# Keys and queries of the later sequence blocks made in seven products per pair of tiles, with the projections in front of the mixers

## The chip, the cores and the metric

One Trainium2 chip; the kernel runs on one of its cores. The metric is the device time of one execution in microseconds. Three runs of the kernel before gave 523.54, 523.78 and 524.24 us; their median, 523.78 us, is the time before.

## What is computed

A sequence `x` of S = 2048 rows and D = 512 columns is normalized row by row (`xn`). Two branches read `xn`.

The first is linear attention with 32 heads of 16 columns. `q`, `k`, `v` are `xn @ wqkv`; `phi(t)` is `t + 1` where `t > 0` and `exp(t)` elsewhere, plus 1e-6:

```python
kv  = einsum("bhsd,bhse->bhde", phi(k), v)
z   = phi(k).sum over s
o   = (phi(q) @ kv) / (phi(q) . z + 1e-6)
s   = o @ wo
```

The second is a token mixer followed by an MLP: `h = gelu(layernorm(xn) @ w1)`, the four quarters of `h`'s columns are shifted by +1, -1, +2 and -2 rows, `x1 = xn + shifted @ w2`, and `x1 + gelu(layernorm(x1) @ w3) @ w4`, with F = 1376 inner columns. The output is `x + s * silu(second branch)`.

## The kernel before

**Tiles and stages.** The rows are cut into 16 tiles of 128 (`NT`), four tiles to a block (`QT = 4`, `NQ = 4` blocks). Each operand of a matrix product is held as a high part rounded to fp32r and a low remainder (`rounds`, `rounded`, L443 and L478), and a product of two operands is three matmuls, high-high, high-low and low-high (`products`, L470). A full-width matmul streams 512 columns.

The stages are, by the names of the tiles in the trace:

- *Projections.* `key(i)` (L748) makes one tile of keys from the transposed block `u` and the split weights `wk`: 4 chunks of 128 rows x 3 = 12 matmuls of 512 columns into the bank `k`. `feature_k` (L735) subtracts the row mean times the column sums of the weights (`wneg`), forms `phi` on ScalarE and VectorE, splits it, and adds it to the running key sum `zacc` by a DMA from GpSimd's queue. `query(i)` (L761) does the same with `wq` into the bank `q`, where `wq` was centered beforehand (`center`, L565), stores `relu` to DRAM from SyncE's queue (SP) and adds `exp` to it by a DMA from GpSimd's queue. `gram(i)` (L771) multiplies the normalized tile `x` with the key features into four accumulators `g` (12 matmuls).
- *Mixers.* `mix1(b, gg)` (L815, bank `h`, 12 matmuls each) makes a quarter of `gelu(.. @ w1)` for a block; `forms` (L836) makes the operands of the next product; `mix2(i)` (L871) multiplies with `w2` a pair of tiles at a time, in seven half-size products in place of eight (`seven`, L778, banks `pa`, `pb`, `pe`). The seven products share three banks: four of them go into `pb`, with read-outs by ScalarE or VectorE between.
- *Attention matrix*: `kv`, `m`, from `g`, `wv`, `wo`.
- *MLP*: `up_pair` (seven products, L1039), `down` (bank `acc`), and for the attention output `attend` and `attend_pair` (banks `s` and `pas`, `pbs`, `pes`), then `gate` and the store of the output.

**The order of the work.** The main function calls these pieces in program order, but it only records operations (`Plan.add`, L96). `Plan.emit` (L267) then lists them by a planner with a cost for each operation, a due time counted back from the matmul that needs it, a fixed number of buffers per kind (89 pieces `p`, four banks `mm`, four accumulators `acc`) and a rule for how long ahead of its due time an operation may take a buffer (`lead`, `early`). Each engine runs its list in order; semaphores hold it where data is missing. `SOONER` (L1402) is a table of operation numbers with corrections to their due times.

**Around the change**, the recorded order is: the weights `wk`, block 0 transposed, tiles 0 to 3; keys 0 to 3; `wq` centered; queries 0 to 3 and gram 0 to 3; `w1` loaded, centered and split (L1228); key 4. Then for blocks b = 1, 2, 3 (L1238): rows loaded and normalized, key and query of the block's tiles, and between them `mix1`, `forms` and `mix2` of the block *before* it. The mixer of block 3, the attention matrix and the MLP follow. A normalized tile `X[i]` stays in its buffer until `mix2` adds it to the mixer's output from GpSimd's queue (L882).

Of the kernel before, what the change touches and what calls it, by code (L numbers as in the profile page):

```python
# [85 lines left out]
class Plan:  # L86
# [180 lines left out]
    def emit(self, first, lead, reserve, window, ahead, table=()):  # L267
# [20 lines left out]
        while left:  # L288
# [5 lines left out]
            for e, cands in avail.items():  # L294
                picks = []
                low = INF
                for op in cands:
# [11 lines left out]
                    for t in fresh:  # L309
# [84 lines left out]
def linear_attn_gated_by_mixer(  # L394
# [29 lines left out]
    EARLY = (), ()  # L424
    AHEAD = 30.0, 20.0, 10.0, 0.0, 0.0
# [67 lines left out]
    onesr, bmask, tiny, zmore = fixed("onesr", P, F32R), fixed("bmask", P), fixed("tiny", 1), fixed("zmore", 1)  # L493
    hal = fixed("hal", NQ * NC * W)
    mv1, mv2 = fixed("mv1", 2 * NT), fixed("mv2", 2 * NT)
    rs1, rs2, ns1, nm1, nm2, au = (fixed(n, NT) for n in ("rs1", "rs2", "ns1", "nm1", "nm2", "au"))
# [13 lines left out]
    pool(.2, [], tiny.all, lambda: g.memset(tiny.all.get(), TINY))  # L510
    pool(.2, [], zmore.all, lambda: g.memset(zmore.all.get(), S * TINY))
# [84 lines left out]
    def scale_x(lo, n):  # L596

        r = rs1[:, lo:lo + n]
        w = small(f"w{lo}", n).all
        pl.ts(w, var(mv1, lo, lo + n), EPS, None, ALU.add, eng="POOL")  # L600
        power(r, w, n)
        pl.ts(ns1[:, lo:lo + n], r, -1.0, None, ALU.mult, eng="POOL")
        pl.tt(nm1[:, lo:lo + n], means(mv1, lo, lo + n), ns1[:, lo:lo + n], ALU.mult, eng="POOL")
        for i in range(lo, lo + n):
            halves_x(i)
# [129 lines left out]
    def feature_k(i, ps):  # L735
# [7 lines left out]
        pl.act(hi, r, AF.Identity, bias=tiny.all)  # L743
# [15 lines left out]
    pqd = {i: memory(f"pqd{i}") for i in range(NT)}  # L759

    def query(i):  # L761
# [3 lines left out]
        pl.act(by_block(e), by_chunk(ps), AF.Relu, scale=col(ns1, i))  # L765
        pl.act(by_block(r), by_chunk(ps), AF.Relu, scale=col(rs1, i))
        pl.act(e, e, AF.Exp, scale=-1.0)
        pl.soon(pl.store(pqd[i].all, r))
        pl.soon(pl.gather(pqd[i].all, e))

# [100 lines left out]
    def mix2(i):  # L871
# [9 lines left out]
        for k, o in ((i, o1), (i + 2, o2)):  # L881
            pl.gather(o, X[k])  # L882
# [293 lines left out]
    def load_rows(i):  # L1176
        load_x(i)
        mv = mv1[:, 2 * i:2 * i + 2]
        if i >= QT:
# [42 lines left out]
    load_rows(QT)  # L1222
    scale_x(QT, 1)
    gram(1)
    query(2)
    gram(2)
    query(3)
    W1 = Weights("w1", w1)  # L1228
    W1.center(by_dma=True)
    W1.split()  # L1230
    gram(3)
    key(QT)
    pl.load(hal.all, halo.rearrange("p q c -> p (q c)"))
    scale_u(0)
    spread_a(0)
    early_s, early_f = EARLY
    fill = [lambda f=f: make_w4(f) for f in early_f] + [lambda s=s: make_pair(s) for s in early_s]
    for b in range(1, NQ):  # L1238
        t0 = b * QT

        def more(n):
            if b > 1:
                for _ in range(n):
                    if fill:
                        fill.pop(0)()

        for j in range(b == 1, QT):
            load_rows(t0 + j)
        split_halo(b - 1)
        scale_x(t0 + (b == 1), QT - (b == 1))  # L1250
        scale_u(b)
        if b > 1:
            load_u(b, 1)
            key(t0)
        query(t0)
        spread_a(b)
        join_a(b - 1)
        more(2)
        if b == 1:
            pl.early = 20.0  # L1260
            prepare_w2()
            pl.early = 0.0
        for gg in ORDER:
            mix1(b - 1, gg)
        forms(b - 1)
        key(t0 + 1)
        query(t0 + 1)
        more(2)
        gram(t0)
        key(t0 + 2)  # L1270
        mix2(t0 - QT)
        query(t0 + 2)
        more(2)
        gram(t0 + 1)
        key(t0 + 3)
        mix2(t0 - QT + 1)
        query(t0 + 3)
        more(2)
        if b < NQ - 1:
            gram(t0 + 2)  # L1280
            gram(t0 + 3)


    b = NQ - 1
    split_halo(b)
    join_a(b)
    for gg in ORDER:
        mix1(b, gg)
    forms(b)
    gram(NT - 2)  # L1290
    gram(NT - 1)
    WV, WO = Weights("wv", wqkv[2]), Weights("wo", wo)
# [15 lines left out]
    pl.act(by_block(zb), by_chunk(zp), AF.Identity, bias=zmore.all)  # L1308
    mix2(b * QT)
# [8 lines left out]
    mix2(b * QT + 1)  # L1318
# [5 lines left out]
    M = {f"b{h + 1}{d + 1}": halves(f"m_b{h + 1}{d + 1}", in2(MQ[h][d])) for h in range(2) for d in range(2)}  # L1324
    while fill:
        fill.pop(0)()
    turn_y(0)
    load_last()
    load_w4(0, FB - 1)
    load_pair(0)  # L1330
    for b in range(NQ):
# [5 lines left out]
        for n, fs in enumerate(groups):  # L1337
# [11 lines left out]
            if b == 0 and n < QT:  # L1349
                turn_q(n)  # L1350
            if b == 0 and 0 < n <= QT:
                attend(n - 1)
# [29 lines left out]
        else:  # L1382
# [19 lines left out]
    SOONER = (  # L1402
# [5 lines left out]
    )  # L1408
    pl.emit(first=6.0, lead={"p": 9.0, "w": 20.0, "ab": 10.0}, reserve={"p": 8, "w": 1, "ab": 0}, window=9.0,
            ahead=6.0, table=SOONER)  # L1410
# [37 lines left out]
```

## Time and profile before

| what | value |
|---|---|
| device time, median of 3 runs | 523.78 us (523.54 to 524.24) |
| span of the profiled execution, first to last instruction | 522.7 us |
| own device time of the profiled execution | not listed beside its profile; the median is 1.1 us above the span |
| TensorE busy | 516.2 us, 3017 matmul records |
| VectorE, ScalarE, GpSimd busy | 372.6, 327.2, 113.1 us |
| moved by DMA | 100.11 MB, mean 192 GB/s |

The page gives the busy time of each engine, the span in 40 slices, the DMA queues, and the chain of work that ended last. A matmul's record is longer than the spacing of matmuls, because they are pipelined (a 512-column matmul has a record of about 390 ns), so a busy share of 99% hides gaps of up to 0.16 us. The spacing is read from the pieces of the chain: the time of twelve matmuls in a row divided by twelve. All times inside the execution count from the span's start.

### The profile page before, as it was taken

Reading aid. Unit: us, or ns where it says so; the run is one execution under the profiler, and the core shown is the slowest. Engines: PE = TensorE matmul, PEld = TensorE weight load, DVE = VectorE, ACT = ScalarE, POOL = GpSimd, SP = SyncE. Lnnn points to the kernel's source line nnn. Section 1 sums busy time; section 2 is a strip of 40 time slices with the busy share of each in tenths; the row PEclk is TensorE's granted clock in tenths of the full one; section 3 lists DMA queues with packets and bytes.
Section 4 is the critical chain, followed back from the end, with each engine's and each line's share of the span. In section 5 each row is a group of like instructions: output and inputs, shape, how many; then the busy total and the mean of one; then the engine's idle time right before and its main releaser. Section 6 shows DMA issues by size and latency. Waiting matters only on the chain.

```text
span 522.7 us, 8905 instructions
## 1 busy us (share of the span) xinstructions
PE 516.2 (99%) x3017; PEld 447.6 (86%) x3017; DVE 372.6 (71%) x745; ACT 327.2 (63%) x669; POOL 113.1 (22%) x207
## 2 busy tenths in 40 slices
PE   8999999999999999999999999999999999999996
PEld 5777888888888888898999889899899898999985
DVE  5778875658474836999997648796657768397735
ACT  6699876588458846867855756356563356544721
POOL 2378312721273023211200022000040000310000
PEclk9999999999999999999999999999999999999999
DMA  8969838863885369999589859847289581995905
GB/s 247 270 155 233 147 88 216 185 163 97 177 225 141 61 113 237 273 269 279 178 287 252 240 156 210 268 135 205 86 186 299 180 237 52 232 257 158 338 9 120
DMA packets 73856, 100.11 MB, mean 192 GB/s; under 512 B 7908, under 2 KB 31988, under 8 KB 73812
## 3 DMA queue, kind: packets, MB, share of 16 engines
q1 hardware_dynamic: 62724, 79.37, 47.9%
q0 software_dynamic: 11088, 20.19, 24.2%
q8 instruction: 23, 0.38, 0.3%
q14 instruction: 21, 0.17, 0.1%
HBM read 60.33 MB, written 30.81 MB: 174 GB/s over the span
## 4 chain that ended last, share of the span: by engine, by line
PE 93%; DMA 4%; SPq 1%; DVE 0%; ACT 0%; POOL 0%; issue 0%
PE acc L146 23%; PE pb L146 11%; PE h L146 9%; PE g L146 8%; PE q L146 7%; PE k L146 6%; PE pe L146 6%; PE pbm L146 4%; PE pbs L146 3%; DMA w1t<-in_w 3%; PE pa L146 3%; PE pem L146 2%; PE s L146 2%; PE a L146 2%; PE pes L146 2%; PE pam L146 1%
## 5 line engine op out<-in xcount | busy, mean ns | idle before, releaser
L223 POOL DMA_DIRECT2D xo<-x1d x12 | 10.7, 1176 | 166.8 <-ACT xo L167 166.8
L223 POOL DMA_DIRECT2D th<-in_x x14 | 12.2, 902 | 71.8 <-DVE th L199 61.4
L223 POOL DMA_DIRECT2D zacc<-kr x16 | 15.1, 944 | 58.2 <-DVE kr L199 55.1
L223 POOL DMA_DIRECT2D o<-x x16 | 14.6, 928 | 40.6 <-DVE o L189 19.1
L167 ACT ACTIVATE p<-pb 128x256 f32<-128x256 f32 x20 | 7.7, 385 | 24.7 <-PE pb L146 24.5
L223 POOL DMA_DIRECT2D pqd<-qe x16 | 16.5, 1032 | 26.7 <-ACT qe L167 13.5
L167 ACT ACTIVATE gf<-gf 128x256 f32<-128x256 f32 (+1 forms) x40 | 20.6, 522 | 0.8
L199 DVE SCALAR_TENSOR_TENSOR kr<-kt,kr 128x512 f32<-128x512 f32 x16 | 11.1, 692 | 14.0 <-ACT kt L167 13.8
L199 DVE SCALAR_TENSOR_TENSOR kt<-wneg,mv,k 128x512 f32<-128x512 f32 x16 | 11.9, 746 | 12.1 <-PE k L146 11.5
L167 ACT ACTIVATE x<-x,nm,rs 128x512 f32<-128x512 f32 x16 | 12.1, 807 | 10.0 <-POOL nm L189 10.0
L189 DVE TENSOR_TENSOR f_10l<-gf,f_10h 96x512 fp32r<-96x512 f32 x4 | 2.7, 686 | 21.5 <-PE pb L146 21.5
L167 ACT ACTIVATE th<-xo 128x512 f32<-128x512 f32 (+1 forms) x16 | 9.5, 613 | 12.0 <-DVE xo L189 11.6
L167 ACT ACTIVATE p<-pe 128x256 f32<-128x256 f32 x20 | 7.7, 384 | 13.4 <-PE pe L146 13.3
L588 DVE BATCH_NORM_STATS2 st<-o 128x6 f32<-128x512 f32 x16 | 11.0, 686 | 4.9 <-DMA o<-x 4.5
L199 DVE SCALAR_TENSOR_TENSOR th<-th,so 128x512 f32<-128x512 f32 (+1 forms) x17 | 11.0, 659 | 4.1 <-ACT th L167 3.3
L167 ACT ACTIVATE qe<-q,ns 128x512 f32<-128x512 f32 x16 | 10.9, 680 | 4.6 <-PE q L146 4.5
L189 DVE TENSOR_TENSOR gf<-pa,p 128x256 f32<-128x256 f32 x20 | 8.3, 417 | 7.1 <-PE pa L146 6.5
L189 DVE TENSOR_TENSOR gf<-u,pe 128x256 f32<-128x256 f32 x20 | 8.4, 418 | 5.9 <-PE pe L146 5.7
L167 ACT ACTIVATE ht<-ht 128x512 f32<-128x512 f32 x16 | 9.6, 626 | 4.5 <-DVE ht L189 4.5
L199 DVE SCALAR_TENSOR_TENSOR qz<-pq,zb 128x512 f32<-128x512 f32 x16 | 10.9, 684 | 1.7 <-PE acc L146 1.6
L167 ACT ACTIVATE xo<-acc 128x512 f32<-128x512 f32 x12 | 7.2, 599 | 7.7 <-PE acc L146 7.3
L167 ACT ACTIVATE y<-o,nm,rs 128x512 f32<-128x512 f32 x16 | 11.9, 802 | 0.0
(1579 smaller groups left out, 2209.8 us busy)
## 6 DMA issues: line engine op xcount, KB each, us to landing
w_s<-in_w SPq DMA_DIRECT2D x28, 256.0 KB, 5.2
x<-in_x SPq DMA_DIRECT2D x16, 256.0 KB, 4.8
zacc<-kr POOLq DMA_DIRECT2D x16, 256.0 KB, 4.2
pqd<-qr SPq DMA_DIRECT2D x16, 256.0 KB, 4.0
pqd<-qe POOLq DMA_DIRECT2D x16, 256.0 KB, 4.9
o<-x POOLq DMA_DIRECT2D x16, 256.0 KB, 4.5
x1d<-o SPq DMA_DIRECT2D x16, 256.0 KB, 4.9
pq<-pqd SPq DMA_DIRECT2D x16, 256.0 KB, 4.5
```

The costliest lines, as they stand in the source:

```text
L146: lambda: nc.tensor.matmul(out.get(), lhs.get(), rhs.get(), start=start, stop=stop, skip_group_check=more))
L167: nc.scalar.activation(out.get(), src.get(), func, scale=get(scale), **kw)
L189: self.vec(eng, out, [a, b], lambda: self.e(eng).tensor_tensor(out.get(), a.get(), b.get(), op=op), True)
L199: lambda: self.nc.vector.scalar_tensor_tensor(out.get(), a.get(), get(s), b.get(), op0=op0, op1=op1),
L223: lambda: self.nc.gpsimd.dma_start(out.get(), get(src), accum_op=ALU.add), mb=mb)
L588: pl.add("DVE", .62, .69, [xv], [st], lambda: nc.vector.bn_stats(st.get(), xv.get()))
```

## The change

Tiles are paired within a block, i with i + 2. For five pairs, (5, 7), (8, 10), (9, 11), (12, 14) and (13, 15), `pair_kq` replaces two calls of `key` and two of `query`. The pair's rows (two halves) times the joined weights (`wk` over `wq`, two halves) are taken as one two-by-two block product and made by seven products of 6 matmuls each, 512 columns wide, in three banks: four into `pb`, one into `pa`, two into `pe`. Tiles 0 to 3, 4 and 6 keep the old functions.

- `forms_w` makes the four combinations of the weights on VectorE and splits them (8 full-width combinations, 8 roundings on ScalarE, 8 remainders on VectorE). `forms_x(b)` makes the four combinations of a block's transposed rows; for blocks 2 and 3 two of them are loaded and added by DMA.
- In `pair_kq` the read-outs scale and add at once: `p1`, `zi`, `qi`, `qk`, `zk` are one VectorE operation each that reads a bank, `p5` and `u2` one ScalarE operation each. `ci` and `ck` hold `1 - mean` terms made from `wneg` on ScalarE. `phi_k`, `phi_q` form the features with one `exp` and one VectorE minimum and maximum; the query feature is stored by SP alone, with no DMA from GpSimd's queue behind it.
- The projections and `gram` of all blocks but the last three grams come ahead of the first `mix1`; the loading of `w1` moves behind the projections; the mixers follow one block after another, the attention matrix between them.
- Each normalized tile is stored to DRAM (`xnd`, 16 stores on SP), and `mix2` adds it from there.
- Six `w4` slices are made ahead (`EARLY`) and fetched again for block 0, `AHEAD` is larger, `SOONER` is gone, moments of blocks 2 and 3 are taken on ScalarE, and the column order that queries had in their buffers is now put into `wqkv` on the host side of the call.

```diff
-                            s = max(s, op.due + slip - n - t.early)
+                            s = max(s, op.due + slip - n - (t.early if len(q) > 16 else 0.0))
...
-    EARLY = (), ()
-    AHEAD = 30.0, 20.0, 10.0, 0.0, 0.0
+    EARLY = (), (10, 0, 5, 1, 6, 2)
+    AHEAD = 100.0, 90.0, 70.0, 30.0, 10.0
...
         rounded(hi, lo, X[i])
+        pl.soon(pl.store(xnd[i].all, X[i]))
         GK[i] = (hi, lo)
...
+    def forms_x(b, j0=0, by_dma=False):
...
+        if by_dma:
+            src = xt[b].rearrange("c p n -> p c n")
+            for n, (lo, cs) in ((0, (h, (TH, BT))), (2, (0, (0, TH)))):
+                pl.load(in2(t[n]), src[:, :h, TH:])
+                pl.gather(in2(t[n]), src[:, lo:lo + h, cs[0]:cs[1]])
...
+    def pair_kq(i):
...
+        ci, ck = piece(f"ci{i}"), piece(f"ck{i}")
+        for t, n in ((ci, i), (ck, k)):
+            pl.act(t, wneg.all, AF.Identity, scale=col(mr1, n), bias=one)
+        go(pb, "a11", "b11")
+        pl.stt(p1, pb, ri, ci, ALU.mult, ALU.add)
+        go(pa, "a12", "b21")
+        pl.stt(zi, pa, ri, p1, ALU.mult, ALU.add)
+        go(pe, "s1", "t1")
+        copy(p5, pe, rk)
+        go(pb, "s2", "t2", False)
+        copy(u2, pb, ri)
+        phi_k(i, zi)
+        go(pe, "s4", "b22", False)
+        pl.stt(qi, pe, ri, u2, ALU.mult, ALU.add)
+        go(pb, "s3", "t3", False)
+        pl.stt(qk, pb, rk, p5, ALU.mult, ALU.add)
+        phi_q(i, qi)
+        go(pb, "a22", "t4", False)
+        pl.stt(zk, pb, rk, ck, ALU.mult, ALU.add)
+        phi_q(k, qk)
+        phi_k(k, zk)
...
+    def phi_k(i, z):
+        e = piece(f"ke{i}")
+        pl.act(e, z, AF.Exp, bias=neg1)
+        pl.stt(e, e, 1.0, z, ALU.min, ALU.max)
+        hi, lo = rounds(f"k{i}")
+        pl.act(hi, e, AF.Identity, bias=tiny)
+        pl.stt(lo, e, TINY, hi.f32, ALU.add, ALU.subtract)
+        pl.gather(zacc.all, e)
+        GK[i] += (hi, lo)
+
+    def phi_q(i, z):
+        e, r = piece(f"qe{i}"), piece(f"qr{i}")
+        pl.act(e, z, AF.Exp, bias=neg1)
+        pl.stt(r, e, 1.0, z, ALU.min, ALU.max)
+        pl.soon(pl.store(pqd[i].all, r))
...
-            pl.gather(o, X[k])
+            pl.gather(o, xnd[k].all)
...
     for b in range(1, NQ):
         t0 = b * QT
...
+        if b > 1:
+            pair_kq(t0)
+        else:
+            for i in (t0, t0 + 2):
+                key(i)
+                query(i)
+        if b > 1:
+            gram(t0 - 3)
+            gram(t0 - 1)
+        if b < NQ - 1:
+            load_u(b + 1, 1)
+            for j in range(QT):
+                load_rows(t0 + QT + j)
+            scale_x(t0 + QT, QT)
+            forms_x(b + 1, by_dma=True)
+        pair_kq(t0 + 1)
...
+        gram(t0)
+        gram(t0 + 2)
...
-    SOONER = (
...
```

More of the change, by code (lines that the diff above doesn't have):

```diff
@@ L1221, in linear_attn_gated_by_mixer, with more @@
     load_u(1, 1)
-    load_rows(QT)
-    scale_x(QT, 1)
+    for i in range(QT, 2 * QT):
+        load_rows(i)
     gram(1)
     query(2)
+    forms_w()
     gram(2)
     query(3)
-    W1 = Weights("w1", w1)
-    W1.center(by_dma=True)
-    W1.split()
     gram(3)
[L1232 to L1235, printed above, removed]
+    scale_x(QT, QT)
+    forms_x(1, 1)
     early_s, early_f = EARLY
+    def more(n):
+        for _ in range(n):
+            if fill:
+                fill.pop(0)()
     fill = [lambda f=f: make_w4(f) for f in early_f] + [lambda s=s: make_pair(s) for s in early_s]
@@ L1239, in linear_attn_gated_by_mixer @@
         t0 = b * QT
[L1241 to L1250, printed above, removed]
+        if b > 1:
[14 more added lines that the diff above has]
+        pair_kq(t0 + 1)
+        if b == NQ - 1:
+            W1 = Weights("w1", w1)
+            W1.center(by_dma=True)
+            W1.split()
+        gram(t0)
+        gram(t0 + 2)
+    pl.load(hal.all, halo.rearrange("p q c -> p (q c)"))
+    for b in range(NQ):
         scale_u(b)
[L1252 to L1255, printed above, removed]
         spread_a(b)
[L1257 to L1286, printed above, removed]
-    for gg in ORDER:
-        mix1(b, gg)
-    forms(b)
-    gram(NT - 2)
-    gram(NT - 1)
+        split_halo(b)
+    join_a(0)
+    for gg in ORDER:
+        mix1(0, gg)
+    forms(0)
+    more(2)
+    prepare_w2()
+    gram(NT - 3)
+    gram(NT - 1)
+    join_a(1)
+    for gg in ORDER:
+        mix1(1, gg)
+    forms(1)
+    more(2)
     WV, WO = Weights("wv", wqkv[2]), Weights("wo", wo)
@@ L1307, in linear_attn_gated_by_mixer @@
     zb = piece("zb")
-    pl.act(by_block(zb), by_chunk(zp), AF.Identity, bias=zmore.all)
-    mix2(b * QT)
+    pl.act(by_block(zb), by_chunk(zp), AF.Identity, bias=zmore)
+    mix2(0)
+    mix2(1)
+    b = 2
+    join_a(b)
+    for gg in ORDER:
+        mix1(b, gg)
+    more(2)
+    mix2(QT)
     kvt = piece("kvt")
```

98 lines of the change are left out of this document (83 added, 15 removed), and 5 rows, old and new, of the table SOONER.

## The prediction

> **What bounds the kernel now.** I read the page first (span, busy times, the granted clock, the chain), then the chain of waits in order of time, then the waits of the weight-load row, then stretches by windows.
>
> ```profile
> span 522.7 us, 8905 instructions
> PE 516.2 (99%) x3017; PEld 447.6 (86%) x3017; DVE 372.6 (71%) x745; ACT 327.2 (63%) x669; POOL 113.1 (22%) x207
> PEclk9999999999999999999999999999999999999999
> PE 93%; DMA 4%; SPq 1%; DVE 0%; ACT 0%; POOL 0%; issue 0%
> ```
>
> TensorE is busy all the time at full clock, and 93% of the chain that ends last is its own work. A kernel in that state gets shorter by what leaves TensorE's list, and longer by every wait that is put into the list.
>
> ```profile
> 39.95 2.79 PE q L146 x12
> 46.37 2.78 PE k L146 x12
> 52.16 11.12 PE h L146 x48
> ...
> 110.00:165.00 55.00, 55.00 (x280) 46.20 (x279) 34.20 (x69) 37.47 (x66) 18.58 (x38) 1.00 0.66 159
> ```
>
> The pieces of the chain give the price: twelve 512-column matmuls of a key or query tile take 2.78 to 2.79 us, 0.232 us each, and 48 of the mixer take 11.12 us, the same. The window (length, then busy us of PE, PEld, DVE, ACT, POOL, clock, DMA share, GB/s) shows the stage that changes: in 55 us of projections and mixers TensorE never pauses, VectorE is busy 34 us and ScalarE 37 us.
>
> **What leaves TensorE.** Two keys and two queries are 4 x 12 = 48 matmuls; seven products are 7 x 6 = 42, of the same width. The instruction order of the changed kernel bears it out: 1275 full-width matmuls become 1245, and the half-width ones stay at 1690. Five pairs x 6 x 0.232 us = **6.97 us** less. The rest of the tiles keep the old form.
>
> The Trainium skill ("TensorE: Matmul & The Clock Gate", section "Back-to-back issue gap") gives an isolated spacing of N/2.4 + 2.5 ns, 216 ns at 512 columns, and about 131 ns in a sustained stream of weight loads and matmuls. By the first the term would be 6.5 us, by the second 3.9 us; the trace has 232 ns, so the measurement decides.
>
> **What comes in, on the other engines.** Per pair VectorE gets five read-outs of banks and six other operations where it had six, so 5 more; ScalarE has 10 where it had 12. Added once: the weights' combinations (16 on VectorE, 8 on ScalarE) and, per block, combinations and roundings of the transposed rows.
>
> ```profile
> L199 DVE SCALAR_TENSOR_TENSOR kt<-wneg,mv,k 128x512 f32<-128x512 f32 x16 | 11.9, 746 | 12.1 <-PE k L146 11.5 <-ACT wneg L167 0.6
> L167 ACT ACT_TABLE_LOAD x8 | 10.3, 1283 | 0.9 <-PEq L1439 0.8
> ```
>
> A bank read by VectorE takes 0.75 us. With 11 operations of about 0.7 us per pair, two pairs, and some 10 us of splits and forms (12 full-width remainders and four half-width sums), a block costs VectorE near 26 us; its matmuls (two pairs and four grams, 132 x 0.232) take 30.6 us. So VectorE fits, but it goes from 62% to 85% and is cover no longer in surplus. As all `exp` now stands ahead of all `gelu`, the order holds 2 table loads in place of 8; these 6 x 1.28 us come off ScalarE, beside TensorE's work, and I count them as nothing.
>
> **What waits it adds.** Inside a pair the banks change hands. A handover in the present seven products looks like this:
>
> ```profile
> 297.92 0.28 PE L146 MATMUL pb<-yt30h,w_s1l 128*128 128x256 f32 x1
> 297.93 0.68 DVE L189 TENSOR_TENSOR yb111l<-y_0t,yb111h 128x512 fp32r<-128x512 f32 x1
> 298.53 0.42 DVE L189 TENSOR_TENSOR gf<-pb,p 128x256 f32<-128x256 f32 x1
> 299.00 0.39 PE L146 MATMUL pb<-yt40h,w_b 128*128 128x256 f32 x1
> 299.23 0.28 PE L146 MATMUL pb<-yt40l,w_b 128*128 128x256 f32 x1
> ...
> PEld pb L146 <- DVE gf L189: 3.0, 10, 0.3
> ```
>
> The sixth product ends at 298.20, VectorE is in a split until 298.53, reads for 0.42 us, and the seventh starts at 299.00; four `acc` matmuls cover the time, and the first matmul after the wait keeps the array 0.23 us where 0.12 is usual. In a pair of the changed kernel the read (`qk`) is 0.75 us, and five `g` matmuls stand between: from the start of the last matmul 0.39 (its record) + 0.75 + 0.05 = 1.19 us are needed, and 6 x 0.232 = 1.39 us are there. That holds with VectorE free, and is 0.4 us short if a split of 0.6 us is ahead of it. In the last pair, (13, 15), only the matmul of `w1`'s mean and one `g` stand between, 0.9 us in all: 0.3 to 0.9 us short. The other handovers have a product of 1.39 us or more as cover. Per pair 0 to 0.5 us, the last one 0.3 to 0.9; I take 0.3 x 4 + 0.6 = **1.8 us**, the middle, because VectorE is at 85% there.
>
> The Trainium skill ("PSUM — Partial Sum Buffer", section "Summary: rules for kernel authors") asks for a different bank when a matmul runs while a bank is being read, and four products in one bank are against that. The row above shows the handover mostly covered; the rival below is what it gives if it is not.
>
> Second, the first pair of blocks 2 and 3 needs `ci`, which needs the row statistics of the whole block. Between the last square sum of the block and `ci`, ScalarE's list has 13 activations.
>
> ```profile
> 25.38 0.62 ACT L167 ACTIVATE wq_2h<-wq_s 128x512 fp32r<-128x512 f32 x1
> 25.90 0.62 ACT L167 ACTIVATE wq_3h<-wq_s 128x512 fp32r<-128x512 f32 x1
> 26.42 0.71 ACT L167 ACTIVATE kr<-kt,rs 128x512 f32<-128x512 f32 x1
> ...
> 30.07 0.71 ACT L167 ACTIVATE k1h<-kr,tiny 128x512 fp32r<-128x512 f32 x1
> 30.68 0.71 ACT L167 ACTIVATE kr<-kt,rs 128x512 f32<-128x512 f32 x1
> ```
>
> Plain copies follow each other every 0.52 us, scaled ones every 0.61. Six copies and seven scaled ones are 7.4 us; in the same stretch of the order TensorE has 33 matmuls, 7.7 us, and then wants `p1`, which takes VectorE another 0.75 us plus the handover. If ScalarE enters the stretch in step, TensorE stands 0.9 us; if ScalarE is ahead, not at all. Twice 0 to 0.9; I take **1.2 us** for both, nearer the upper end.
>
> **The head.** `SOONER` moved early operations, and without it the first loads and activations stand in another order: `x0` and its two sums now stand behind the first weights and rows.
>
> ```profile
> 5.03 0.63 ACT L167 ACTIVATE sq<-x 128x512 f32<-128x512 f32 x1 [1.43 <-DMA x<-in_x]
> 5.97 0.72 ACT L167 ACTIVATE sq<-x,sx 128x512 f32<-128x512 f32 x1 [0.22 <-DVE sx L194]
> 6.69 0.40 ACT L167 ACTIVATE u_0h<-xt 128x256 fp32r<-128x256 f32 x1
> 9.49 0.42 PE L146 MATMUL k<-wk_0l,u_0h 128*128 128x512 f32 x1
> ...
> 28.68 0.82 ACT L167 ACTIVATE x<-x,nm,rs 128x512 f32<-128x512 f32 x1 [0.79 <-POOL nm L189]
> ...
> PEld g L146 <- ACT k1h L167: 0.8, 1, 0.8
> ...
> 30.00:35.00 5.00, 4.45 (x19) 3.08 (x18) 3.14 (x6) 4.97 (x9) 4.49 (x9) 1.00 0.30 77
> ```
>
> The two sums hold `u_0h` back by up to 1.3 us, and the matmuls run without gaps from 9.49 on: up to 1.3 us to gain. Against it, ScalarE is full at 30 to 35 us while TensorE waits 0.55 us, for `k1h`; in the changed list 16 activations stand between `k0h` and `k1h` where 11 stood, 5 x 0.6 = 3 us more, of which its idle moments take some (0.8 in the row of 28.68): up to 2.2 us to lose. From -1.3 to +2.2; I take **+0.4**, the middle.
>
> **DMA and the later stages.** Sixteen stores, 8 transfers for the rows' combinations and 12 fetches of `w4` come in, 10 additions of `exp` go: 26 more of 256 KB, about 6.7 MB on 100 MB. SP's queue is passed by these stores too; it already stands for such stores:
>
> ```profile
> SPq L210 <- ACT qr L167: 118.8, 16, 14.4
> ...
> w_s<-in_w SPq DMA_DIRECT2D x28, 256.0 KB, 5.2
> ...
> DMA packets 73856, 100.11 MB, mean 192 GB/s; under 512 B 7908, under 2 KB 31988, under 8 KB 73812
> ```
>
> In the changed order the loads stand at least 7 us of matmuls ahead of their use outside the head and one query tile (5 in the order of before), and a load takes about 5 us to land, so I count them as covered. VectorE is full where the MLP begins, in both orders:
>
> ```profile
> 216.00:240.00 24.00, 24.00 (x157) 20.77 (x156) 23.57 (x51) 18.55 (x43) 3.56 (x4) 1.00 1.00 265
> 260.00:300.00 40.00, 40.00 (x267) 36.43 (x266) 32.25 (x66) 24.71 (x54) 0.00 (x0) 1.00 0.92 268
> ```
>
> Its work there is the same within an operation or two: -0.5 to +0.8 us, I take **+0.2**.
>
> **The sum.** -6.97 + 1.8 + 1.2 + 0.4 + 0.2 = -3.4 us: a span of 522.7 - 3.4 = 519.3 us, and with the 1.1 us by which the median stands above the span, **520.4 us**.
>
> **The rivals.**
>
> *All waits are covered.* VectorE and ScalarE run ahead, as in the window of 55 us above, where neither was over 70%. Then only the matmuls count, with a head that comes out even: 523.8 - 6.97 = 516.8 us. Against it stands VectorE's 26 of 30.6 us.
>
> *The waits eat the gain.* The seventh product stands bare in each pair: 0.39 + 0.75 = 1.1 us, five times, and ScalarE's 0.9 us twice: 7.3 - 6.97 = +0.3, 524.1 us, no change that can be told. It needs VectorE over an operation behind at each `qk`; against it speaks that the present handovers wait 0.3 us at most.
>
> *Slower, by DMA.* In the order, the 40 us of matmuls in which the last mixers and the first MLP products lie issue 12.0 MB; the densest such stretch of before issues 10.5 MB. Full DMA engines moved 265 to 268 GB/s (rows above): 12.0 MB take 45 us, 5 us longer than the matmuls. Loads of `w3` and `w4` then come late at the first products. It decides as soon as the lag is more than the lead less the landing, 7 - 5 = 2 us. 520.4 + 5 = 525.4 us. Many of these transfers are stores that nobody waits for, which speaks against it.
>
> That the change doesn't do what it says can be left out: 30 matmuls are gone from the list, and the list is what the kernel waits for.
>
> **How the numbers follow.** The forecast 0.47 (its own range 517.7 to 522.5), all covered 0.20, eaten 0.18, slower 0.15. A measurement of this kernel tells about 0.2% (1.05 us) from no change. Faster by more: 0.47 + 0.20 and a little of "eaten", 0.70; within: 0.14; slower: 0.16. The range goes from 516.0, "all covered" with part of the gain of the head, to 525.0, short of the worst of the slower case.
>
> **What would show it.** Right: rows `pbx`, `pax`, `pex` whose products keep 1.39 us per six matmuls; waits of PE or PEld on `pbx` for VectorE, about 0.3 us a time, and on `p1` in the first pair of blocks 2 and 3; two table loads; TensorE still over 98% busy. Wrong: waits of over 1 us at each `pbx`; waits for DMA in the first MLP products or DMA share at 1.00 over more than 40 us; TensorE's wait for `k1h` over 2 us; or no waits at all in the pairs.

## The result, and the profile after

The changed kernel takes 525.77 us (median of 14 runs, 524.71 to 527.22) against 523.89 us of the kernel before (14 runs beside them): 1.0033 times as long, 95% interval 1.0024 to 1.0042. The forecast was 520.4 us with a range of 516.0 to 525.0 us, so the measured time lies above both. The change is slower by 0.3%, although it takes 30 matmuls out of the list that sets the time.

The first part of the page of the changed kernel, and the shares of its chain by engine:

```profile
span 524.8 us, 9024 instructions
PE 511.2 (97%) x2987; PEld 441.9 (84%) x2987; DVE 403.8 (77%) x822; ACT 336.3 (64%) x705; POOL 112.5 (21%) x202
PE 71%; ACT 5%; DVE 3%; DMA 3%; issue 1%; DVEq 0%; ACTq 0%
```

TensorE has 30 instructions less, as forecast. But where 99% of the span was busy it is 97%, and the chain, 93% TensorE before, now runs through ScalarE and VectorE in places. The span is 2.1 us longer, so something like 9 us of waiting has come in. Where it lies is shown by the same windows of both kernels (length, then busy us of PE, PEld, DVE, ACT, POOL, clock, DMA share, GB/s). Before:

```profile
55.00:135.00 80.00, 80.00 (x407) 67.18 (x407) 52.92 (x106) 55.85 (x99) 23.52 (x44) 1.00 0.63 148
135.00:240.00 105.00, 105.00 (x567) 88.80 (x566) 74.53 (x154) 73.32 (x139) 31.11 (x53) 1.00 0.79 194
240.00:280.00 40.00, 40.00 (x280) 36.85 (x279) 38.95 (x81) 29.63 (x66) 2.98 (x4) 1.00 0.79 242
```

After:

```profile
55.00:135.00 80.00, 77.23 (x325) 59.83 (x324) 62.44 (x122) 68.35 (x127) 35.06 (x64) 1.00 0.84 214
135.00:240.00 105.00, 104.35 (x628) 91.03 (x627) 92.02 (x199) 71.84 (x155) 17.70 (x24) 1.00 0.78 211
240.00:280.00 40.00, 37.96 (x256) 34.13 (x255) 38.69 (x81) 26.66 (x56) 5.73 (x10) 1.00 0.87 264
```

Before, these windows show no pause of TensorE in 225 us. After, it pauses in the pairs (55 to 135 us) and where the MLP begins (240 to 280 us). In the pairs ScalarE went from 56 to 68 of 80 us; in the mixers, which now stand alone, VectorE went from 75 to 92 of 105 us.

To close the account I added up, stage by stage, how much later each matmul starts than the one ahead of it plus its usual pitch (0.232 us for 512 columns, 0.118 for 256, 0.428 for the few in full precision). This is the waiting, in us:

| stage (us of the span) | before | after | difference | the prediction had |
|---|---|---|---|---|
| head, 0 to 55 | 6.68 | 6.71 | 0.0 | +0.4 |
| pairs, 55 to 135 | 0.34 | 4.69 | +4.4 | +3.0 |
| mixers, 135 to 240 | 0.64 | 2.31 | +1.7 | |
| start of the MLP, 240 to 280 | 0.53 | 3.31 | +2.8 | +0.2 for all of these |
| 280 to 460 | 2.38 | 1.73 | -0.7 | |
| from 460 | 1.17 | 2.10 | +0.9 | |
| sum | 11.74 | 20.86 | +9.1 | +3.6 |
| matmuls at their usual pitch | 505.03 | 498.07 | -7.0 | -7.0 |

Together +2.1 us, which is the difference of the two spans. The waits of TensorE themselves, in the view that names the releaser, the instruction that ended the wait (waited for; us in total, times, longest):

```profile
PE pb L146 <- DVE gf L189: 1.4, 3, 0.6
PE pbx L146 <- DVE p1x L199: 1.3, 1, 1.3
PE acc L146 <- DVE f_0l L189: 1.1, 1, 1.1
...
PE pbx L146 <- ACT u2x L167: 0.9, 1, 0.9
PE h L146 <- ACT ar L167: 0.7, 1, 0.7
PE pex L146 <- ACT p5x L167: 0.4, 1, 0.4
```

None of these is directly on a DMA. Three belong to the pairs (`p1x`, `u2x`, `p5x`), one to the first mixer (`ar`), two mostly to the start of the MLP (`gf`, `f_0l`). The longest wait of the pairs, in the timeline (start, length, engine, instruction, and in brackets the idle time before it and its releaser):

```profile
72.01 0.75 POOL L194 TENSOR_SCALAR ns<-rs 128x4 f32<-128x4 f32 x1
72.85 0.48 POOL L189 TENSOR_TENSOR nm<-mv,ns 128x4 f32<-128x4 f32 x1
73.29 0.64 POOL L189 TENSOR_TENSOR mr<-mv,rs 128x4 f32<-128x4 f32 x1
73.36 2.94 ACT L167 ACTIVATE x<-x,nm,rs 128x512 f32<-128x512 f32 x4 [0.16 <-POOL nm L189]
76.19 0.39 PE L146 MATMUL pex<-kq_t11h,xs_0l 128*128 128x512 f32 x1
76.21 0.80 ACT L167 ACTIVATE ci<-wneg,few,mr 128x512 f32<-128x512 f32 x1
77.04 0.75 DVE L199 SCALAR_TENSOR_TENSOR p1x<-pbx,rs,ci 128x512 f32<-128x512 f32 x1 [1.89 <-ACT ci L167]
77.84 0.50 PE L146 MATMUL pbx<-kq_t20h,xs_1h 128*128 128x512 f32 x1 [1.26 <-DVE p1x L199]
```

The third product ends, and the fourth needs the bank that `p1x` has yet to read. `p1x` waits for `ci`, and `ci` stands in ScalarE's list behind four normalised rows that take 2.94 us. From 76.19 to 77.84 are 1.65 us where 0.23 is usual: 1.42 us lost. ScalarE ran without a pause there; the releaser that the view names, VectorE, was idle for 1.89 us itself.

The next one, 1.05 us ahead of the sixth product of pair (9, 11), has a longer chain behind it:

```profile
93.14 0.75 DVE L199 SCALAR_TENSOR_TENSOR zi<-pax,rs,p1x 128x512 f32<-128x512 f32 x1 [0.98 <-DMA pqd<-qr]
94.41 0.68 DVE L189 TENSOR_TENSOR x10l<-x,x10h 128x512 fp32r<-128x512 f32 x1
95.18 0.64 ACT L167 ACTIVATE sq<-x 128x512 f32<-128x512 f32 x1 [0.80 <-DVE x10l L189]
...
96.42 0.76 ACT L167 ACTIVATE u2x<-pbx,few,rs 128x512 f32<-128x512 f32 x1
97.23 0.50 PE L146 MATMUL pbx<-kq_t30h,xs_2h 128*128 128x512 f32 x1 [0.89 <-ACT u2x L167]
```

`u2x`, the read-out that frees the bank, stands in ScalarE's list behind two row sums (`sq`) of the next block. The first of them waits until VectorE has made `x10l`, and VectorE had waited 0.98 us ahead of `zi`, by the view for the store of a query feature (`pqd`). So ScalarE stood idle here for 0.80 us: this wait comes from the place of the sums in the list, and a store stands at the far end of the chain.

At the start of the MLP:

```profile
248.52 0.64 ACT L167 ACTIVATE f_0h<-gf 128x512 fp32r<-128x512 f32 x1 [0.42 <-DVE gf L189]
251.06 1.30 DVE L155 STREAM_TRANSPOSE y_0z<-y 128x512 f32<-128x512 f32 x2
252.28 1.33 DVE L155 STREAM_TRANSPOSE y_1z<-y 128x512 f32<-128x512 f32 x2
...
258.47 2.46 DVE L591 BATCH_NORM_STATS2 st<-o 128x6 f32<-128x512 f32 x4
260.85 0.67 DVE L189 TENSOR_TENSOR f_0l<-gf,f_0h 128x512 fp32r<-128x512 f32 x1
...
261.57 0.73 PE L146 MATMUL acc<-w_0h,f_0l 128*128 128x512 f32 x2 [1.10 <-DVE f_0l L189]
```

`f_0h` is made at 248.5, its remainder `f_0l` only at 260.9. In between VectorE makes, among other things, transposes and row statistics of blocks 2 and 3, 5 us of work that TensorE needs only when those blocks reach the MLP.

### The profile page after: what moved, and what is told of

It reads as the page before. It is cut to its first block, busy times and chain, and to the rows that moved or that the text cites. A ratio compares the mean times of both kernels' runs of the same rounds, so it can differ in the third digit from the quotient of the medians.

```text
span 524.8 us, 9024 instructions
## 1 busy us (share of the span) xinstructions
PE 511.2 (97%) x2987; PEld 441.9 (84%) x2987; DVE 403.8 (77%) x822; ACT 336.3 (64%) x705; POOL 112.5 (21%) x202
## 4 chain that ended last, share of the span: by engine, by line
PE 71%; ACT 5%; DVE 3%; DMA 3%; issue 1%; DVEq 0%; ACTq 0%
PE acc L146 22%; PE pb L146 10%; PE h L146 9%; PE pe L146 5%; PE pbm L146 4%; PE pbs L146 3%; PE pa L146 2%; PE pem L146 2%; PE g L146 2%; PE a L146 2%; DMA xo<-x1d 2%; PE s L146 2%; PE pes L146 2%; PE pbx L146 1%; DMA pqd<-qr 1%; PE pam L146 1%
## 5 line engine op out<-in xcount | busy, mean ns | idle before, releaser
L223 POOL DMA_DIRECT2D xo<-x1d x12 | 10.7, 1133 | 155.8 <-ACT xo L167 155.8
L223 POOL DMA_DIRECT2D o<-xnd x16 | 14.0, 916 | 59.1 <-DVE o L189 44.9
L223 POOL DMA_DIRECT2D zacc<-ke x10 | 9.3, 925 | 30.8 <-DMA zacc<-ke 12.6
L194 POOL TENSOR_SCALAR w<-mv 128x4 f32<-128x4 f32 (+2 forms) x10 | 2.9, 290 | 54.0 <-DVE mv L592 39.3
L189 DVE TENSOR_TENSOR ht<-h,abc 128x512 f32<-128x512 f32 x16 | 10.9, 688 | 2.3 <-PE h L146 1.7
L189 DVE TENSOR_TENSOR so<-so,xo 128x512 f32<-128x512 f32 (+1 forms) x16 | 10.5, 670 | 1.0 <-DMA xo<-x1d 0.9
L199 DVE SCALAR_TENSOR_TENSOR pq<-pq,rd 128x512 f32<-128x512 f32 x16 | 11.0, 688 | 0.1
L167 ACT ACTIVATE u<-pb 128x256 f32<-128x256 f32 x20 | 7.7, 383 | 5.4 <-PE pb L146 5.4
L189 DVE TENSOR_TENSOR gf<-pb,p 128x256 f32<-128x256 f32 x20 | 8.4, 422 | 3.2 <-PE pb L146 2.4
```

What stands on the lines that cost most here:

```text
L167: nc.scalar.activation(out.get(), src.get(), func, scale=get(scale), **kw)
L189: self.vec(eng, out, [a, b], lambda: self.e(eng).tensor_tensor(out.get(), a.get(), b.get(), op=op), True)
L194: lambda: self.e(eng).tensor_scalar(out.get(), a.get(), get(s1), get(s2), **kw), False,
L199: lambda: self.nc.vector.scalar_tensor_tensor(out.get(), a.get(), get(s), b.get(), op0=op0, op1=op1),
L223: lambda: self.nc.gpsimd.dma_start(out.get(), get(src), accum_op=ALU.add), mb=mb)
```

## The experiments

The theories: **lists** (the products save what they should, and the loss is work that stands in the wrong order, or is too much, in the lists of ScalarE and VectorE), against **products** (the seven products cost their gain through their own chain of banks), **DMA** (the added transfers) and **table** (the loss is the old table of due times, dropped by the change). Some kernels keep the changed kernel's order of issue, whole or up to a time (40 or 132 us of the plan), by a list of operations that the planner must follow, so that an edit does not reshuffle what lies ahead of it. Ratios are to the kernel before, run on the same chip. Times of different chips differ by some tenths of a us; so the changed kernel was run again as r7:

> The changed kernel itself, its planner replaced by the list of instructions that it planned, for a comparison on the same chip. Every theory: 525.0 to 526.5 us, 1.0033 of the kernel before.

526.97 us, above the expected 525.0 to 526.5; ratio 1.0045 (1.0032 to 1.0058), and the interval overlaps the first one. Its waits by stage are 6.88, 4.93, 2.29, 3.30, 1.82, 2.33, the same picture.

**r1, the old table alone.**

```diff
-            ahead=6.0, table=SOONER)
+            ahead=6.0)
```

> The kernel before, with only its table of moved due times (SOONER) taken out. Two theories. (a) Part of what the change lost is the table, which was made for the old list of operations and was dropped with it: the head has matmuls that wait at 20 to 45 us for wq and the first x and k halves, and this kernel is 1.5 to 3 us slower than the kernel before (525.4 to 526.9 us). (b) The table is worth nothing on the chip: 523.4 to 524.4 us, and the whole loss lies in the pairs and the new order.

524.56 us, ratio 1.0012 (1.0000 to 1.0025): about 0.6 us, below what (a) wanted and not clearly above nothing. The table is not where the loss is.

**r2, the order without the products.**

```diff
-        if b > 1:
-            pair_kq(t0)
-        else:
-            for i in (t0, t0 + 2):
-                key(i)
-                query(i)
+        for i in (t0, t0 + 2):
+            key(i)
+            query(i)
...
-        pair_kq(t0 + 1)
+        for i in (t0 + 1, t0 + 3):
+            key(i)
+            query(i)
```

(and without `forms_w` and `forms_x`)

> The changed kernel with the five pairs made tile by tile again (two keys, two queries, 48 matmuls), and without the combinations of weights and rows; the order of the stages is kept, and the first 40 us are issued in the order of the changed kernel. (a) The seven products take 6.97 us off TensorE and give back about 4.3 us in waits inside the pairs: this kernel is 2 to 3.5 us slower than the changed one (527.8 to 529.3 us). (b) The waits come from the order of the stages and not from the products: it is 6 to 7.5 us slower (531.8 to 533.3 us), and the waits at 60 to 130 us stay. (c) The products give nothing: within 1 us of the changed kernel.

527.65 us, ratio 1.0072 (1.0055 to 1.0090), 1.4 us by the ratios above r7; the intervals just overlap. So as they stand the products are worth 1 to 2 us, not 7, a little below the range of (a), and the new order without them would be slower than the kernel before by 3.8 us. Its windows:

```profile
55.00:135.00 80.00, 80.00 (x344) 64.43 (x343) 35.46 (x57) 58.61 (x98) 34.46 (x69) 1.00 0.85 196
240.00:280.00 40.00, 38.21 (x257) 34.44 (x256) 38.80 (x82) 27.01 (x57) 5.72 (x10) 1.00 0.91 267
```

Tile by tile TensorE does not pause from 55 to 135 us, so those waits come with the pairs; but the pause at the start of the MLP stays, so it comes with the order. There are two losses, with two causes.

**r3, the stores of the rows left out.** Stores and the dependence stay in the plan, only the transfers are not issued, and the mixers add rows of `x` in place of the normalised ones, so the output is not the reference's.

```diff
-        pl.soon(pl.store(xnd[i].all, X[i]))
+        pl.soon(pl.add("SP", .42, 0, [X[i]], [xnd[i].all], lambda: None, mb=512 * P * 4 / 1e6))
...
-            pl.gather(o, xnd[k].all)
+            pl.add("POOL", .8, 0, [xnd[k].all, o], [o], lambda o=o, k=k: nc.gpsimd.dma_start(
+                o.get(), x[k * P:(k + 1) * P, :], accum_op=ALU.add), mb=512 * P * 4 / 1e6)
```

> The changed kernel, in the same order of instructions, without the 16 stores of the normalised rows (4.2 MB); the additions in the mixers read the rows of the input in their place, so the result is not the reference's. (a) The wait of 1.05 us at the fourth product of the second pair of block 2, and those of VectorE for stores of pqd (1.0 and 1.5 us), come from stores that land late because these 16 stand in the same queue: 1 to 2 us faster than the changed kernel (523.8 to 524.8 us), and these waits are gone. (b) The stores are hidden, and the waits come from the engines' lists: within 0.6 us of it.

526.63 us, ratio 1.0046 (1.0028 to 1.0064): (b), as r7. No wait of VectorE is named after a store of `pqd` any more, but `zi` starts no earlier (93.65 us, 93.14 in the changed kernel), and the wait on `u2x` in the second pair of block 2 is 1.48 us, no shorter; it lies ahead of the sixth product, not of the fourth as the expectation has it. So the 16 stores, 4.2 of the 6.7 MB added, cost nothing that can be told. The other added transfers were not taken out.

**r4, `ci` ahead of the four rows.** In the list of the changed kernel `mr` is moved ahead of `ns` and `nm`, and `ci` ahead of the four `x`, in blocks 2 and 3; nothing else is moved.

> The changed kernel with two moves in blocks 2 and 3: GpSimd makes the mean times the reciprocal deviation ahead of the two other products, and ScalarE makes ci ahead of the four normalised rows. (a) The wait of 1.42 us before the fourth product of pair 8 is ci behind those four rows (2.9 us of ScalarE): it is gone, and the kernel is 1.2 to 1.6 us faster than the changed one (524.2 to 524.6 us). (b) ScalarE and VectorE are full there and the wait comes back a few products later: within 0.5 us of it.

527.03 us, ratio 1.0049 (1.0032 to 1.0066): (b). The timeline at the same place:

```profile
72.42 0.81 ACT L167 ACTIVATE ci<-wneg,few,mr 128x512 f32<-128x512 f32 x1
73.27 2.94 ACT L167 ACTIVATE x<-x,nm,rs 128x512 f32<-128x512 f32 x4
74.38 0.74 DVE L199 SCALAR_TENSOR_TENSOR p1x<-pbx,rs,ci 128x512 f32<-128x512 f32 x1
...
77.16 0.76 ACT L167 ACTIVATE p5x<-pex,few,ns 128x512 f32<-128x512 f32 x1
...
77.97 0.50 PE L146 MATMUL pex<-wq_2h,xs_3h 128*128 128x512 f32 x1 [0.68 <-ACT p5x L167]
```

`p1x` is in time now, 2.7 us earlier, and its wait is gone. One product later the same four rows hold back `p5x`, and TensorE stands there for 0.83 us. The waits of the pairs fall from 4.93 to 3.91 us in all, and those at the start of the MLP rise from 3.30 to 4.90, with a new one of 1.53 us on `pb` that was not followed up. A stall named and removed was only the first in a queue.

**r6, less work on ScalarE.**

```diff
-        if QT <= i < 2 * QT:
+        if i >= QT:
             moments(f"st{i}", X[i], mv)
```

> The changed kernel with the row statistics of blocks 2 and 3 on VectorE again (two instructions a row) in place of two square sums on ScalarE; the first 40 us are issued in the order of the changed kernel. (a) ScalarE, busy 68 of 80 us from 55 to 135 us, is what makes the read-outs u2 and p5 and the term ci late: with 8 to 10 us less there the waits of 1.42, 1.05 and 0.52 us shrink to 1 us or less together, and the kernel is 1.5 to 2.5 us faster than the changed one (523.3 to 524.3 us). (b) The waits are those of the order of the lists, not of a full engine: within 0.8 us of the changed kernel, with as much waiting at 60 to 130 us.

522.96 us, ratio 0.9980 (0.9968 to 0.9991): 3.4 us better than r7 by the ratios, more than (a) had.

```profile
55.00:135.00 80.00, 79.02 (x337) 62.16 (x336) 67.69 (x118) 60.84 (x100) 34.74 (x65) 1.00 0.84 214
```

ScalarE is busy 60.8 us of the 80 in place of 68.4, VectorE 5 us more, and the waits of the pairs fall from 4.93 to 1.95 us. The change had moved the row statistics of two blocks to ScalarE: sixteen instructions, a sum and a square sum for each of eight tiles of rows, in the very stretch where ScalarE reads out banks. (Behind the first 40 us the list of r6 was planned anew, so other work has moved as well.)

**r13, another order for ScalarE.** Is it the amount of work, or the place of the four rows in the list? The patience of a store is a number of the planner: how long after the TensorE work of its time it may be made. Work that only the store needs gets its due time from it.

```diff
+        pl.patience = 30.0
         pl.soon(pl.store(xnd[i].all, X[i]))
+        pl.patience = 18.0
```

> The changed kernel with one number changed: the stores of the normalised rows get 30 us of patience in place of 18, so that the four rows of a block no longer stand ahead of ci, p5 and u2 in ScalarE's list; the square sums stay on ScalarE, and the first 40 us are issued in the order of the changed kernel. (a) The order of ScalarE's list alone makes the waits of the pairs: TensorE's waits from 55 to 135 us fall from 4.7 to 4.9 us to 2.5 us or less, and the kernel is 2 us or more faster than the changed one (under 525 us, ratio under 1.001). (b) ScalarE has too much to do there, whatever the order (it is busy 68 of 80 us): the waits stay above 3.5 us and move to other products, and only less work, as in r6, helps.

525.62 us, ratio 1.0033 (1.0021 to 1.0045): (b). Waits for `p1x` are gone here as well, and those for `p5x` take their place (window, and waits of TensorE):

```profile
55.00:135.00 80.00, 77.42 (x327) 60.23 (x326) 62.09 (x122) 69.27 (x127) 36.20 (x65) 1.00 0.82 214
```

```profile
PE pex L146 <- ACT p5x L167: 2.1, 3, 1.4
```

The waits of the pairs stay at 4.11 us. Moving one group of ScalarE's work, by hand (r4) or by its due time (r13), moves the wait; taking the row statistics off ScalarE (r6) took away more than half of the waiting.

**r5, patience for the MLP's rows.** Here the patience sets when VectorE makes the statistics and transposes of the blocks whose MLP comes later.

```diff
             if soon:
+                if self.name[0] == 'y' and int(self.name[1]) >= 1:
+                    op.patience = 45.0
                 pl.soon(op)
```

> The changed kernel with one number changed: the stores of the turned rows of the MLP's input for blocks 1 to 3, and with them the row statistics and transposes that they need, get 45 us of patience in place of 18 in the planner; the first 132 us are issued in the order of the changed kernel. (a) The waits at 240 to 280 us (on f_0l 1.26, on pb 0.75 and 0.52 us) are VectorE standing in work of blocks 2 and 3 that nobody needs yet, next to mixers that no longer lie between projections: they go, and the kernel is 2 to 3 us faster than the changed one (522.8 to 523.8 us). (b) VectorE has too much to do there altogether: the waits move on by some us, less than 1 us gained.

523.48 us, ratio 0.9989 (0.9978 to 1.0001): (a), 2.9 us better than r7 by the ratios.

```profile
240.00:280.00 40.00, 40.00 (x278) 36.96 (x277) 38.53 (x83) 25.80 (x57) 5.28 (x9) 1.00 0.85 257
```

VectorE is as busy there as before the edit (38.5 of 40 us), and TensorE does not pause any more: the waits fall from 3.30 to 0.58 us. Here it was the order, not the amount.

**r8 to r12, lists fitted to the work.** r8 has the patience of r5 for all blocks, two costs in the planner corrected by the trace, and a table of eleven moved due times that was searched, by the plan's own end, for this list of operations.

```diff
+        if isinstance(scale, View) and isinstance(bias, View):
+            lat += .1
...
-            lat = (.3 if n <= 8 else .15 + n / (435 if pair else 1000))
+            lat = (.5 if n <= 8 else .15 + n / (435 if pair else 1000))
...
+    SOONER = (
+        55, 50, 68, 25, 73, 43, 83, 28, 202, 26, 646, 64, 782, 44, 2044, 27, 4561, 12, 4654, 19, 4786, -38,
+    )
```

> The changed kernel with the patience of 45 us, with the planner told what the trace shows (ScalarE's instructions with a scale and a bias column 0.1 us longer, GpSimd's smallest 0.5 us in place of 0.3), and with a new table of eleven moved due times for its own list of operations. (a) What the products saved was lost to lists that nobody had fitted to them: the waits of the pairs shrink to the handovers (1.8 us), those at the start of the MLP and of the head go, and the kernel takes 517.5 to 520.5 us, faster than the kernel before. (b) The waits of the pairs are in the products themselves: 521.5 to 523.5 us, of which the start of the MLP gives 2 to 3 us.

518.61 us, ratio 0.9892 (0.9880 to 0.9905): (a), faster than the kernel before by 1.1%.

```profile
55.00:135.00 80.00, 78.44 (x334) 61.60 (x333) 67.12 (x124) 68.97 (x122) 34.96 (x63) 1.00 0.83 208
```

Its waits by stage are 5.62, 2.53, 1.37, 0.32, 2.08, 1.20. In the pairs ScalarE does as much as in the changed kernel (69.0 us) and half of the waits are gone: the whole list fitted does what one moved group (r4, r13) does not. So a busy ScalarE alone does not make the waits: less work (r6) or a better order of all lists (r8) takes them down.

Is this the products, or would fitting help any order? r9 fits the kernel before in the same way (costs, and a table searched from its own one), r10 undoes the products in r8:

> The kernel before given the same fitting as r8: the two costs of the planner corrected and its table of due times searched anew. (a) TensorE already does without waits there, so nothing is left to fit: 522.8 to 524.2 us, and what r8 gained belongs to the products. (b) The fitting gives to any order of the work: 2 us or more faster than the kernel before (under 522.2 us).

> r8 with the five pairs made tile by tile (48 matmuls for 42) and without the combinations; the first 40 us are issued in the order of r8, patience and costs are kept. (a) With the lists fitted the products give 6.97 us less what waits are left in the pairs of r8 (3.3 us from 55 to 135 us): 3.3 to 5 us slower than r8 (521.9 to 523.6 us). (b) The products give little whatever the lists: under 2.5 us slower than r8 (under 521.1 us). (c) The waits of r8 there are not the pairs': 6.5 us slower or more (over 525 us).

r9: 524.73 us, ratio 1.0008 (0.9995 to 1.0021), nothing gained. r10: 523.99 us, ratio 0.9996 (0.9983 to 1.0010), 5.4 us slower than r8 by the ratios, somewhat more than (a) had. No table was searched for r10's own list; but its waits, counted as in the table of stages, are 10.7 us in all against 13.1 in r8 and 11.4 in r15 below, so a search would have had little to take.

```profile
55.00:135.00 80.00, 80.00 (x346) 64.50 (x345) 35.94 (x60) 58.36 (x101) 34.51 (x65) 1.00 0.86 193
```

So the products are worth about 5.4 of their 7.0 us once the lists fit. The waits that are left in the pairs (2.53 us against none) are more than the rest.

r11 puts the statistics on VectorE and r12 takes the new table out again:

> r8 with the row statistics of blocks 2 and 3 on VectorE and a table searched for that list. (a) ScalarE is what delays the read-outs: the 3.3 us of waits from 55 to 135 us in r8 shrink by 1 us or more, 516.5 to 517.8 us. (b) With fitted lists ScalarE is ahead anyway: 518 to 519.2 us, as r8.

> r8 without its table of eleven moved due times; patience and the two corrected costs stay. (a) The table is worth what it takes out of the head (the wait of the first g for x0h, about 2.4 us by the plan) and of pair 8 (p1, about 1.5 us): 521.8 to 523 us. (b) It is worth little on the chip, as the old table of the kernel before was (r1: 0.6 us): 518.6 to 520 us.

r11: 518.78 us, ratio 0.9897 (0.9884 to 0.9910), (b): with a fitted list the edit of r6 gives nothing more. r12: 528.09 us, ratio 1.0067 (1.0044 to 1.0090), 9 us slower than r8, far beyond (a). Its list has waits of more than 2 us at three places, and each costs 1.6 to 1.8 times its length, as the last section shows.

**r14 and r15, rows late in the fitted kernels.**

> r8 with the 30 us of patience for the normalised rows and a table searched for that list. By (a) the waits of r8 on p5 (0.66 and 1.22 us) go: 516.5 to 517.7 us. By (b) others take their place: 518 to 519 us, as r8.

> r11 (row statistics of blocks 2 and 3 on VectorE) with the 30 us of patience and a table searched for that list. Both theories: 516 to 518 us, since here neither the order nor the amount of ScalarE's work should hold the read-outs; above 518.5 us both are incomplete.

r14: 518.97 us, ratio 0.9913 (0.9888 to 0.9937). Three of its six runs take 517.40 to 517.78 us and three 520.16 to 521.45 us, so it does not decide between (a) and (b); a wait of 0.8 us on `p5x` is still in its profile. r15: 517.17 us, ratio 0.9875 (0.9862 to 0.9887), the best version, 6.6 us faster than the kernel before; waits 5.02, 2.05, 1.17, 0.40, 2.10, 0.62.

```profile
span 515.3 us, 9007 instructions
PE 507.4 (98%) x2987; PEld 440.4 (85%) x2987; DVE 407.4 (79%) x814; ACT 327.6 (64%) x673; POOL 114.7 (22%) x202
```

## Why the prediction was wrong

*What leaves TensorE, 6.97 us:* right. The matmuls at their usual pitch add up to 6.96 us less, and the six of a product that nothing holds up take 1.38 to 1.40 us.

*The handovers inside the pairs, 1.8 us:* too large. The wait that was priced, of the seventh product for VectorE's `qk`, is there in two pairs, 0.25 and 0.40 us, 0.65 in all. Two more at `pbx`, 0.20 and 0.31 us, stand ahead of the sixth product, where the prediction saw "a product of 1.39 us or more as cover". The weight loads' row names ScalarE for these two and the 1.05 us above:

```profile
PEld pbx L146 <- ACT u2x L167: 2.4, 3, 1.3
```

*Late inputs, 1.2 us:* too small; with these 3.5 us (1.42 on `p1x`, 1.56 on `u2x` in three pairs, 0.52 on `p5x`). The step that failed here is the count of what comes in on ScalarE, "ScalarE has 10 where it had 12", and with it the cover of the banks that ScalarE reads. The count left out the row statistics that the change puts on ScalarE for blocks 2 and 3, sixteen instructions of 0.6 to 0.7 us, and the prediction looked for the bound on VectorE. ScalarE became the fullest engine beside TensorE there (68 of 80 us). With these instructions off ScalarE (r6) 3.0 of the 4.93 us of waiting are gone; r4, r8 and r13 show that the order of the lists decides where it appears and how much of it. For `ci` the form was foreseen, but only with ScalarE in step or ahead. In the first pair of block 2 it was late: the prediction's 33 matmuls (7.7 us) counted back from 76.42 us, where the fourth product was due, give 68.8 us, and the last square sum ends at 69.27. By this estimate 0.5 us of lag came on top of the 0.9. That `u2` and `p5` stand in the same list was not foreseen.

*The head, +0.4 us:* the stage waits as long as before, within the 0.9 us by which it differs from one profile of the same list to another (6.88 us in r7, 6.03 in r4, whose list is the same there).

*DMA, nothing:* right as far as the runs go. r3 takes 4.2 MB out and changes nothing, and behind the head TensorE has no long wait on a DMA; in one chain, that of `u2x` in pair (9, 11), a store stands further back.

*The later stages, +0.2 us:* this is the step that failed most, 4.7 us. "Its work there is the same within an operation or two" is true of VectorE's total, and the busy time in the window is the same (38.95 and 38.69 of 40 us). What was not looked at is which work stands in that list when. Before, projections lay between the mixers, VectorE had room there (75 of 105 us), and the statistics and transposes of a block were made on the way. With the projections in front the mixers fill it (92 of 105), and the planner's patience of 18 us, which fitted the old order, drops the rows of blocks 2 and 3 in front of the first MLP products. r2 shows that the order does this without the pairs, r5 that the patience does it. So 2.8 of the 4.7 us are explained. The wait at the first mixer (`ar`), 0.90 us by the count of the table, is 0.27 us in r2; about 1 us more in the mixers is there in r2 too, so it comes with the order, and was not followed further.

*The rivals:* the time lies by "slower, by DMA" (525.4), but only by chance: behind the head TensorE waits for no DMA longer than 0.2 us. What happened is nearer to "the waits eat the gain" (524.1), with ScalarE in the place of VectorE and a second loss outside the pairs that no rival had.

*The signs:* two table loads, 1.39 us per product and small waits on `pbx` came as said. TensorE at 97% in place of over 98%, and a wait for `p1x` of 1.3 us in one first pair and none in the other, did not. One sign of being wrong came without its cost: the DMA share is 1.02 to 1.07 in each 20 us from 190 to 250 us. In r5 it is 0.97 to 1.06 there, and the waits at the start of the MLP are gone.

What stays open: the 0.9 us by which the waits from 460 us on are longer. They are 2.33 us in r7 and 1.48 us in r4, whose list is the same there; 0.60 us of them is one wait on `pb` at 465.9 us (0.82 in r7, none in r4), and no run was made for them.

## What to carry to other kernels

When TensorE work is taken out of a full list, count every instruction that the change puts on each other engine in that stage, those of moved helpers too, and compare the busy time with the stage's new length: the engine that fills up there (ScalarE here, 68 of 80 us) is where to look for late reads. When stages are put one behind the other that used to alternate, ask which engine the alternation had relieved, and which due times and costs in the planner were fitted to it; the same totals in another order cost 3 us here, and one number gave them back. A large change in a planned kernel is measured fairly only with its plan fitted anew: unfitted the seven products were worth 1 to 2 us, fitted about 5.4.

## What the runs showed of the hardware

**A wait of about 2 us can cost more than itself.** In r12 TensorE waits ahead of the fourth product of pair 8 (timeline, and a window of the same place, where the clock is the column behind the engines):

```profile
77.47 0.40 PE L146 MATMUL pex<-kq_t11h,xs_0l 128*128 128x512 f32 x1
80.22 0.53 PE L146 MATMUL pbx<-kq_t20h,xs_1h 128*128 128x512 f32 x1 [2.35 <-DVE p1x L201]
80.55 0.63 PE L146 MATMUL pbx<-kq_t20l,xs_1h 128*128 128x512 f32 x1
80.98 0.63 PE L146 MATMUL pbx<-kq_t20h,xs_1l 128*128 128x512 f32 x1
```

```profile
82.00:84.00 2.00, 2.00 (x7) 1.52 (x6) 0.94 (x2) 1.29 (x3) 1.74 (x4) 0.51 1.07 139
```

After 2.35 us of idle time the matmuls start every 0.43 us in place of 0.23, until 83.96: the granted clock is half, and nine matmuls take 3.74 us in place of 2.09. With the wait that is 4.2 us lost, by the count of the stages. The same follows a wait of 3.06 us at 19 us (4.8 us lost) and one of 2.07 us at 294 us (3.7 us lost); it follows none of the 1.26 us of the changed kernel, nor one of 1.41 us in r13. The Trainium skill ("TensorE: Matmul & The Clock Gate", section "What's actually happening") has the clock halved after an idle window of about 3.4 us and back after as long a busy one. The second agrees with the trace; for the first, 2.07 us were enough here. The clock records of the trace show more: the three stretches at half clock begin at 22.51, 80.54 and 295.58 us and last 3.413 us each, and 58.03 and 215.04 us, the times between them, are 17 and 63 times 3.413 us. So in this run the clock seems to change only at fixed moments, 3.413 us apart. Of the 3.41 us before each change 3.06, 2.35 and 1.90 us were idle; for the 1.41 us of r13, which lay in one such stretch by the same reckoning, the clock stayed. What a wait costs thus seems to depend on where it falls and not on its length alone.

**Two column operands on ScalarE.** Four `x<-x,nm,rs`, with a scale and a bias column, take 2.94 us, 0.71 us each, where a plain copy takes 0.52; the planner had 0.61. The Trainium skill ("ScalarE: Activation LUTs", section "What ACT_TABLE_LOAD costs") gives about 93 ns for each such operand, and the trace agrees.

**The first matmul behind a wait** starts the next one 0.33 to 0.34 us later in place of 0.23 (80.22 to 80.55 above), and at 256 columns 0.22 in place of 0.12. It is so for all fourteen waits of TensorE in the changed kernel behind the first 12 us: each costs about 0.1 us beside its length.
